# A decode step of attention plus a gated MLP on one core: the weight rows of `w_out` laid five to a lane on 128 lanes, and the remaining rows ten to a lane on 24 lanes

## The chip, the core and the metric

One NeuronCore of one Trainium2 chip. The core has a matrix engine (PE, with its weight loads PEld), a vector engine (DVE), a scalar engine (ACT), GpSimd (POOL) and SyncE (SP), which here only issues transfers. Sixteen DMA engines move data between HBM and the on-chip memory of 128 lanes. The metric is the device time of one execution in microseconds: before the change the median of three runs is 662.51 us (662.46 to 662.76).

## The reference, cut to what matters

```python
x = A_x                                   # (4, 1, 640)
xn = layernorm(x)
out = x + A(xn, k_cache, v_cache, wq, wo) + B(xn, w_in, w_sp, b_sp, w_out)

# A: attention of one new token over a cache, batch 4, 32 heads, 4096 positions, head size 128
q = (xn @ wq) by heads
p = softmax(q . k_cache * 128**-0.5)
A = (p @ v_cache) by heads, flattened, @ wo

# B: gated MLP, Fh = 864
z  = gelu(xn @ w_in)                      # w_in is 640 x 1728
z1 = z[..., :864];  z2 = layernorm(z[..., 864:])
B  = (z1 * (w_sp * z2 + b_sp)) @ w_out    # w_out is 864 x 640
```

All inputs are bf16. The two caches hold 268 MB; all weights together hold 14 MB.

## The kernel before

**Tiles.** The caches are cut into 16 tiles each, `i` = 0 to 15 (a group of eight heads and one batch). Such a tile is 128 lanes of 32768 bf16 numbers, 8.39 MB: K tiles have two buffers (`kp`), V tiles have one (`vp`). Below, K0 is the first K tile, V0 the first V tile, and so on. The weights use the same buffers: `wq` takes the first K buffer's turn, and `w_sb` the V buffer's first turn. `w_sb` holds `w_in` (columns 0 to 8639 of each lane) and behind it `w_out`.

**Transfers.** All large transfers are issued by SP, on one queue, in one order: `w_out` (L109), `wq` (L114), `w_in` (L121), four small transfers for the rest of `w_out` (L123), K0 (L139); then K1, V0 (L145) and the later tiles in turn, and `wo` (L159) last. A tile's transfer is issued when its buffer is free: K(i+2) when the PE has summed the second half of K(i) (`sums(i, 1)`, L475), V(i) when `weighted(i-1)` (L568) has read the V tile before. V0 takes the buffer of `w_sb`, so it is issued only when the MLP has used `w_out` for the last time.

**The MLP.** `gmlp()` runs once, before the loop over the tiles. It multiplies `w_in` by the transposed `xn` into `zT` (L317, 70 matmuls), applies gelu and the layernorm on DVE and ACT, and ends in `yT` (L405): seven blocks of up to 128 rows by 4 batches. Then `add_out` (L216) adds `yT` times `w_out` into `out_ps`, with four matmuls of 160 columns for each block. For this, row f of `y` must lie on the lane on which row f of `w_out` lies. The first 768 rows of `w_out` lie six to a lane (row 6p + k on lane p); `w_in`'s columns are read with a stride of six to match. The other 96 rows lie six to a lane on 16 lanes, loaded in four transfers of four lanes each; `yT`'s last block is turned to that layout by six matmuls with parts of the unit matrix (`ye_ps`, L408) and one copy (`yE`, L416).

**The loop.** For each tile, DVE multiplies a half of K(i) by q (`product`, L449), adds the two halves of the head size (`fold`, L463), and PE sums the rest into `s_ps` (`sums`, L475). DVE reduces it (L486), finds the maxima, ACT takes the exponentials (L542), DVE spreads them (`pm`, L553), and PE multiplies them by V (L568).

**Order.** From `stage_q(0)` and `gmlp()` on, the code stands in a block whose order is kept as written for PE, DVE, ACT and SP (`tc.manual_schedule`): all of `gmlp()` stands ahead of `product(0, 0)` on DVE and ahead of `sums(0, 0)` on PE. What stands ahead of that block, the loads of the weights and of K0 among it, is put in order by the framework's scheduler, which may change the order of the text. Waits are inserted by the framework, by the regions of the tiles that an instruction reads and writes.

Of the kernel before, what the change touches and what calls it, by code (L numbers as in the profile page):

```python
# [17 lines left out]
def kernel(  # L18
# [14 lines left out]
    nc = tc.nc  # L33
    P = nc.NUM_PARTITIONS
# [4 lines left out]
    Fh = F // 2  # L39
# [14 lines left out]
    SLOT = NC * Dh  # L54
# [9 lines left out]
    WJ = WH * Dh // P  # L64
    WW = 2
    WR = NG * ROWS
    NFF = Fh // P
    TL = 16
    TK = (Fh - NFF * P) // TL
    TE = 4  # L70
    NFC = NFF + TK
    F0 = NFF * P
    TF = TL * TK
    NZ = NFF + 1
    assert F0 + TF == Fh and TF <= P
    NQ = 4
    NO = D // NQ
    REP = GW // Bsz
# [18 lines left out]
    def v_slot(name):  # L97
# [8 lines left out]
    w_sb = v_slot("w_sb")  # L106
    w_in_sb = w_sb[:, 0 : DC * F].rearrange("p (c n) -> p c n", c=DC)
    w_out_sb = w_sb[:, DC * F : DC * F + NFC * D].rearrange("p (k n) -> p k n", k=NFC)
    nc.sync.dma_start(  # L109
        out=w_out_sb[:, 0:NFF, :], in_=B_w_out[0 : NFF * P].rearrange("(p k) n -> p k n", k=NFF)  # L110
# [11 lines left out]
    for l in range(TL // TE):  # L122
        nc.sync.dma_start(  # L123
            out=w_out_sb[:TL, NFF:NFC, :].rearrange("(e l) k n -> e l (k n)", e=TE)[:, l],
            in_=B_w_out[F0:Fh].rearrange("(e l k) n -> e l (k n)", e=TE, k=TK)[:, l],
        )

    def kv_view(cache, i):
# [34 lines left out]

    ident = const.tile([P, P], BF16)
    make_identity(nc, ident[:])
    ident_f = const.tile([P, P], FP32)
    nc.gpsimd.tensor_copy(out=ident_f[:], in_=ident[:])
    eps_tile = const.tile([P, 1], FP32)
# [13 lines left out]
    for i in range(NSTAT):  # L182
# [5 lines left out]
        out=rstd[:], in_=mv[:, 1:2], func=ACT.Sqrt, bias=eps_tile[:Bsz], scale=1.0  # L188
# [3 lines left out]
        out=xn_bf,  # L192
# [9 lines left out]
    for c in range(DC):  # L202
        nc.tensor.transpose(
            out=xnT_ps[:, c, :], in_=xn_v[:, c, :], identity=ident[:Bsz, :Bsz]
# [3 lines left out]
        out=xnT_r[:], in_=xnT_ps[:, :, :, None].to_broadcast([P, DC, Bsz, REP])  # L208
# [5 lines left out]
    def add_out(lhsT, rhs, start=False, stop=False):  # L214
# [14 lines left out]
        out=own[:], in_=ident_f[:].rearrange("p (h l) -> p h l", h=HT), axis=AX.X, op=ALU.add  # L229
# [4 lines left out]
        out=pick[:, :, GW - HT : GW],  # L234
        in_=ident_f[:].rearrange("p (j h c) -> p c h j", c=CB, h=HT),
# [5 lines left out]
        out=row_head_f[:],  # L241
        in_=ident_f[:WR, :WR].rearrange("p (g b h) -> p g h b", g=NG, h=HT),
# [5 lines left out]
        out=row_head[:],  # L248
        in_=row_head_f[:].rearrange("p g h -> p (g h)")[:, :, None].to_broadcast([WR, WH, WL]),
# [3 lines left out]
        out=row_batch_f[:],  # L253
        in_=ident_f[:WR, :WR].rearrange("p (g b h) -> p b g h", g=NG, h=HT),
# [12 lines left out]
    for t in range(2):  # L267
        for c in range(DC):
            for j in range(CG):
                n = CG * t + j  # L270
                nc.tensor.matmul(  # L271
                    out=q_ps[t][GW * j : GW * (j + 1), :],
                    lhsT=xnT_r[:, c].rearrange("p b r -> p (b r)"),
                    rhs=wq_t[:, c, n * NW : (n + 1) * NW],
                    start=(c == 0),
                    stop=(c == DC - 1),
                )
        nc.scalar.copy(out=q_rows[:, t, :], in_=q_ps[t][:])
    for t in range(2):
        qT_ps = ps_m.tile([P, HQ, CG, Bsz, REP], BF16, tag="m", name="qT_ps")  # L280
        for n in range(HQ):
            nc.tensor.transpose(  # L282
                out=qT_ps[:, n].rearrange("p j b r -> p (j b r)"),
                in_=q_rows[:, t, n * Dh : (n + 1) * Dh],
# [24 lines left out]
    def gmlp():  # L309
        zz, gw, gt, gz, sq = (gm[n] for n in ("zz", "gw", "gt", "gz", "sq"))  # L310
        zT = ps_pv.tile([P, 2, NZ, Bsz], FP32, tag="pv", name="zT")
        for t in range(2):
            f1 = t * Fh + F0
            w_t = w_in_sb[:, :, t * Fh : f1].rearrange("p c (f k) -> p c k f", k=NFF)
            for k in range(NZ):
                for c in range(DC):
                    nc.tensor.matmul(  # L317
                        out=zT[: P if k < NFF else TF, t, k, :],
                        lhsT=w_t[:, c, k, :] if k < NFF else w_in_sb[:, c, f1 : f1 + TF],
                        rhs=xnT[:, c, :],  # L320
                        start=(c == 0),
                        stop=(c == DC - 1),
                    )
        nc.vector.tensor_copy(out=zz[:, :, 0:NFF, :], in_=zT[:, :, 0:NFF, :])
        nc.vector.tensor_copy(out=zz[:TF, :, NFF:NZ, :], in_=zT[:TF, :, NFF:NZ, :])
        nc.vector.tensor_tensor(out=gw, in0=zz, in1=zz, op=ALU.mult)
        nc.vector.tensor_scalar(
            out=gw, in0=gw, scalar1=0.044715, scalar2=1.0, op0=ALU.mult, op1=ALU.add
        )
        nc.vector.tensor_tensor(out=gw, in0=gw, in1=zz, op=ALU.mult)  # L330
        nc.scalar.activation(
            out=gt, in_=gw, func=ACT.Tanh, scale=math.sqrt(2.0 / math.pi)
        )
        nc.vector.tensor_scalar(
            out=gt, in0=gt, scalar1=1.0, scalar2=0.5, op0=ALU.add, op1=ALU.mult
        )
        nc.vector.tensor_tensor(out=gz, in0=zz, in1=gt, op=ALU.mult)
        nc.vector.tensor_tensor(out=sq, in0=gz[:, 1, :, :], in1=gz[:, 1, :, :], op=ALU.mult)

        s_ps = ps_m.tile([1, 2, NZ, Bsz], FP32, tag="m", name="ln_ps")  # L340
        for n, src in enumerate((gz[:, 1, :, :], sq)):
            nc.tensor.matmul(
                out=s_ps[:, n, :, :], lhsT=ones_col[:], rhs=src, start=True, stop=True
            )
        st, ac = gm["st"], gm["ac"]
        mean_t = st[:, 0:Bsz]
        ex2_t = st[:, Bsz : 2 * Bsz]
        var_t = st[:, 2 * Bsz : 3 * Bsz]
        rst_t = st[:, 3 * Bsz : 4 * Bsz]
        tmp_t = st[:, 4 * Bsz : 5 * Bsz]  # L350
        nc.vector.tensor_reduce(
            out=st[:, 0 : 2 * Bsz].rearrange("a (n b) -> a n b", b=Bsz),
            in_=s_ps[:].rearrange("a n k b -> a n b k"),
            axis=AX.X,
            op=ALU.add,
        )
        nc.vector.tensor_scalar(
            out=st[:, 0 : 2 * Bsz],
            in0=st[:, 0 : 2 * Bsz],
            scalar1=1.0 / float(Fh),  # L360
            scalar2=None,
            op0=ALU.mult,
        )
        nc.vector.tensor_tensor(out=tmp_t, in0=mean_t, in1=mean_t, op=ALU.mult)
        nc.vector.tensor_tensor(out=var_t, in0=ex2_t, in1=tmp_t, op=ALU.subtract)
        nc.scalar.activation(
            out=rst_t, in_=var_t, func=ACT.Sqrt, bias=eps_tile[:1], scale=1.0
        )
        wsp_t = work.tile([1, 1], FP32, name="wsp_t")
        nc.vector.tensor_copy(out=wsp_t[:], in_=wsp_bf[:])  # L370
        bsp_t = work.tile([1, 1], FP32, name="bsp_t")
        nc.vector.tensor_copy(out=bsp_t[:], in_=bsp_bf[:])
        nc.vector.reciprocal(out=rst_t, in_=rst_t)
        nc.vector.tensor_scalar(
            out=ac[:, 0:Bsz], in0=rst_t, scalar1=wsp_t[:, 0:1], scalar2=None, op0=ALU.mult
        )
        nc.vector.tensor_tensor(out=tmp_t, in0=ac[:, 0:Bsz], in1=mean_t, op=ALU.mult)
        nc.vector.tensor_scalar(
            out=ac[:, Bsz : 2 * Bsz],
            in0=tmp_t,  # L380
            scalar1=-1.0,
            scalar2=bsp_t[:, 0:1],
            op0=ALU.mult,
            op1=ALU.add,
        )
        ac_ps = ps_m.tile([P, 2 * Bsz], FP32, tag="m", name="ac_ps")
        nc.tensor.matmul(
            out=ac_ps[:], lhsT=ones_row[:], rhs=ac[:], start=True, stop=True
        )
        ac_sb = work.tile([P, 2 * Bsz], FP32, name="ac_sb")  # L390
        nc.scalar.copy(out=ac_sb[:], in_=ac_ps[:])
        nc.vector.tensor_tensor(
            out=sq,
            in0=gz[:, 1, :, :],
            in1=ac_sb[:, None, 0:Bsz].to_broadcast([P, NZ, Bsz]),
            op=ALU.mult,
        )
        nc.vector.tensor_tensor(
            out=sq,
            in0=sq,  # L400
            in1=ac_sb[:, None, Bsz : 2 * Bsz].to_broadcast([P, NZ, Bsz]),
            op=ALU.add,
        )
        yT = work.tile([P, NZ, Bsz], BF16, name="yT")
        nc.vector.tensor_tensor(out=yT[:], in0=gz[:, 0, :, :], in1=sq, op=ALU.mult)  # L405
        ye_ps = ps_m.tile([TL, TK, Bsz], FP32, tag="m", name="ye_ps")
        for k in range(TK):
            nc.tensor.matmul(  # L408
                out=ye_ps[:, k, :],
                lhsT=ident[:TF, :TF].rearrange("p (f k) -> p k f", k=TK)[:, k, :],  # L410
                rhs=yT[:TF, NFF, :],
                start=True,
                stop=True,
            )
        yE = work.tile([TL, TK, Bsz], BF16, name="yE")
        nc.scalar.copy(out=yE[:], in_=ye_ps[:])  # L416
        for k in range(NFC):
            if k < NFF:
                add_out(yT[:, k], w_out_sb[:, k, :])
            else:  # L420
                add_out(yE[:, k - NFF], w_out_sb[:TL, k, :])
# [347 lines left out]
```

## Time and profile before

| what | value |
|---|---|
| median of 3 runs | 662.51 us |
| profiled execution, span | 661.1 us |
| DVE busy | 491.6 us (74%) |
| PE busy | 295.4 us (45%) |
| ACT busy | 34.4 us (5%) |
| POOL busy | 2.1 us |
| moved by DMA | 282.55 MB, mean 427 GB/s |
| `product` L449 | 32 x 8688 ns |
| `fold` L463 | 31 x 4410 ns |
| K tiles, issue to landing, median | 39.6 us |
| V tiles, issue to landing, median | 33.7 us |

The profile is one execution; its span is 1.4 us under the median of the runs. A page of the profile gives busy times, a row of forty slices of the span, the chain of work that ended last, and groups of instructions. The timeline lists instructions by their start; "issue" of a transfer is the instruction on SP, not the movement of data. A landing is the moment when the last byte's completion is seen. In a timeline row the columns are start, duration, engine (SPq is SP's sequencer), line, operation, output <- input, count, and in brackets the idle time before and what ended it.

### The profile page before, as it was taken

The numbers are of one execution on the slowest core, as the hardware profiler recorded it, in microseconds if no ns is written. First come the engines' busy times: TensorE is split into PE (matmuls) and PEld (weight loads), VectorE is DVE, ScalarE is ACT, GpSimd is POOL, SyncE is SP. The second block draws the span as 40 slices with busy tenths as digits, with TensorE's granted clock in tenths as the row PEclk, the third lists the DMA queues.
The fourth block names the chain that finished last, engine by engine and source line by source line (L and its number), as shares of the span: only waits on it lengthen the run. The fifth ranks groups of instructions, "written<-read, shape, count | busy, mean of one in ns | idle before, by whom it ended". The sixth has DMA issues, their size and how long they took to land.

```text
span 661.1 us, 4720 instructions
## 1 busy us (share of the span) xinstructions
PE 295.4 (45%) x2099; PEld 127.9 (19%) x2099; DVE 491.6 (74%) x222; ACT 34.4 (5%) x94; POOL 2.1 (0%) x15
## 2 busy tenths in 40 slices
PE   0513464536426253552625344362634507263656
PEld 0301121212112021220202112120211202031223
DVE  1249999959597795959779569986959699695851
ACT  0300000000000000000000000000000000000000
POOL 1000000000000000000000000000000000000000
PEclk9756676876858687675868757787775768777688
DMA  8999999999999999999999999999999999999996
GB/s 377 456 428 444 428 417 441 429 436 441 436 420 433 432 429 445 440 421 432 424 436 441 440 425 432 420 441 436 437 428 437 425 432 429 440 432 437 432 406 275
DMA packets 5712, 282.55 MB, mean 427 GB/s; under 512 B 680, under 2 KB 812, under 8 KB 1084
## 3 DMA queue, kind: packets, MB, share of 16 engines
q1 hardware_dynamic: 5664, 282.24, 98.9%
q8 instruction: 16, 0.26, 0.2%
q14 instruction: 4, 0.03, 0.0%
q10 hardware_dynamic: 28, 0.01, 0.0%
HBM read 282.24 MB, written 0.01 MB: 427 GB/s over the span
## 4 chain that ended last, share of the span: by engine, by line
DMA 51%; DVE 37%; PE 9%; issue 2%; ACT 1%; SPq 0%; DVEq 0%; ACTq 0%
DMA k_nat<-in_A_k_cache_dram 47%; DVE k_nat L449 22%; DVE k_nat L463 11%; PE s_ps L475 8%; DMA wo<-in_A_wo_dram 4%; DVE s_sb L486 3%; DMA w_sb<-in_B_w_out_dram 1%; ACT p L542 1%; PE pv L568 1%; DVE m L495 1%; PE mT L500 0%; DVE nm L505 0%; DVE pm L553 0%; SPq L159 0%; PE out_ps L216 0%
## 5 line engine op out<-in xcount | busy, mean ns | idle before, releaser
L449 DVE TENSOR_TENSOR k_nat<-k_nat,qbc 128x16384 bf16<-128x16384 bf16 x32 | 278.0, 8688 | 97.8 <-DMA k_nat<-in_A_k_cache_dram 97.8
L475 PE MATMUL s_ps<-k_nat,ident 128*128 128x512 bf16 x528 | 184.8, 528 | 139.3 <-DVE k_nat L463 139.3
L463 DVE TENSOR_TENSOR k_nat<-k_nat 128x8192 bf16<-128x8192 bf16 x31 | 136.7, 4410 | 0.0
L475 PEld LDWEIGHTS <-ident 128*128 128x128 bf16 x528 | 65.3, 129 | 248.3 <-DVE k_nat L463 123.3
L500 PE MATMUL mT<-ident_f,m 128*1 128x128 f32 x16 | 5.9, 366 | 160.0 <-DVE m L495 160.0
L568 PE MATMUL pv<-v_nat,pm 128*32 128x512 bf16 x960 | 56.1, 387 | 0.8 <-DVE pm L553 0.8
L486 DVE TENSOR_REDUCE s_sb<-s_ps 128x128 f32<-128x1024 f32 x32 | 39.0, 1218 | 5.4 <-PE s_ps L475 5.4
L500 PEld LDWEIGHTS mT<-ident_f,m 128*1 128x1 f32 x16 | 1.3, 79 | 167.8 <-DVE m L495 156.2
L568 PEld LDWEIGHTS <-pm 128*32 128x32 bf16 x1024 | 27.1, 100 | 34.3 <-issue 8.5
L553 DVE TENSOR_TENSOR pm<-p,own_c 128x2048 bf16<-128x2048 bf16 x16 | 19.6, 1225 | 15.3 <-ACT p L542 15.3
L542 ACT ACTIVATE p<-s_sb,nb 128x256 bf16<-128x256 f32 x16 | 8.1, 508 | 394.1 <-DVE nb_h L524 394.1
L591 PE MATMUL o_ps<-e,pick 128*32 128x128 f32 x128 | 17.0, 276 | 11.2 <-ACT e L578 11.2
L591 PEld LDWEIGHTS o_ps<-e,pick 128*32 128x32 f32 x128 | 12.7, 109 | 18.7 <-ACT e L578 18.7
L578 ACT COPY e<-pv 128x512 f32<-128x512 f32 x16 | 9.4, 586 | 68.1 <-PE pv L568 60.6
L287 DVE COPY qT<-qT_ps 128x64 bf16<-128x64 bf16 x2 | 0.4, 224 | 15.5 <-PE qT_ps L282 15.5
L516 PE MATMUL nb_ps<-nm,ones_row 1*128 1x8 f32 x32 | 9.2, 359 | 6.0 <-DVE nm L505 6.0
L505 DVE TENSOR_REDUCE nm<-mT 1x8 f32<-1x128 f32 x16 | 4.5, 279 | 7.5 <-PE mT L500 7.5
L516 PEld LDWEIGHTS nb_ps<-nm,ones_row 1*128 1x128 f32 x32 | 7.7, 298 | 10.6 <-DVE nm L505 9.9
L271 PE MATMUL q_ps<-wq,xnT_r 128*32 128x512 bf16 x40 | 4.3, 609 | 11.2 <-DMA wq<-in_A_wq_dram 11.2
L443 ACT CAST qbc<-qbc_ps 128x128 bf16<-128x128 f32 x16 | 4.3, 266 | 92.3 <-PE qbc_ps L435 92.3
L608 PE MATMUL den<-ones_col,acc_h 128*32 128x1 f32 x8 | 1.0, 194 | 16.6 <-DVE acc_h L601 16.6
L495 DVE TENSOR_REDUCE m<-s_sb 128x1 f32<-128x256 f32 x16 | 6.7, 420 | 0.5
(92 smaller groups left out, 70.7 us busy)
## 6 DMA issues: line engine op xcount, KB each, us to landing
wq<-in_A_wq_dram SPq DMA_DIRECT2D x1, 5120.0 KB, 16.3
wo<-in_A_wo_dram SPq DMA_DIRECT2D x1, 2560.0 KB
w_sb<-in_B_w_in_dram SPq DMA_DIRECT2D x1, 2160.0 KB, 20.9
wo<-in_A_wo_dram SPq DMA_DIRECT2D x1, 1760.0 KB
w_sb<-in_B_w_out_dram SPq DMA_DIRECT2D x1, 960.0 KB
wo<-in_A_wo_dram SPq DMA_DIRECT2D x1, 640.0 KB, 25.5
k_nat<-in_A_k_cache_dram SPq DMA_DIRECT2D x16, 39.6
v_nat<-in_A_v_cache_dram SPq DMA_DIRECT2D x15, 33.7
```

The lines of the kernel that those rows point to most:

```text
L449: nc.vector.tensor_tensor(out=part(i, u), in0=part(i, u), in1=qbcs[i][:, None, :].to_broadcast([P, UC, Dh]), op=ALU.mult,)
L463: nc.vector.tensor_tensor(out=t[:, :, 0:HD2], in0=t[:, :, 0:HD2], in1=t[:, :, HD2:Dh], op=ALU.add)
L475: nc.tensor.matmul(out=sums_ps[i][:, c : c + SC], lhsT=ident[:], rhs=t[:, c : c + SC, g * RW : (g + 1) * RW], start=(g == 0), stop=(g == n ...
L486: nc.vector.tensor_reduce(out=scores[i][:, u * UC : (u + 1) * UC], in_=sums_ps[i][:], axis=AX.X, op=ALU.add,)
L495: nc.vector.tensor_reduce(out=m1[:], in_=scores[i][:], axis=AX.X, op=ALU.max)
L500: nc.tensor.transpose(out=mT[:], in_=maxes[i][:], identity=ident_f[:])
L516: nc.tensor.matmul(out=nb_ps[:], lhsT=ones_row[:], rhs=maxes[i][:], start=True, stop=True)
L542: nc.scalar.activation(out=probs[i][:], in_=scores.pop(i)[:], func=ACT.Exp, bias=maxes.pop(i)[:], scale=scale_qk, accum_out=accs[hg][:, b ...
L553: nc.vector.tensor_tensor(out=pm[:], in0=probs.pop(i)[:] .rearrange("p (n c) -> p n c", c=CB)[:, :, None, :] .to_broadcast([P, NB, HT, CB] ...
L568: nc.tensor.matmul(out=pvs[i][j * GW : (j + 1) * GW, :], lhsT=pm[:, n, :, :].rearrange("p h c -> p (h c)"), rhs=v_nat[:, n * CB : (n + 1) ...
L578: nc.scalar.copy(out=es[i][:], in_=pvs.pop(i)[:].rearrange("p (c d) -> p c d", d=Dh))
L591: nc.tensor.matmul(out=o_ps[hg // NG][own_rows(hg), :], lhsT=pick[:, c, GW - HT - HT * b : 2 * GW - HT - HT * b], rhs=e[:, c, :], start=(b ...
```

## The change

Of the 864 rows of `w_out`, 640 lie five to a lane on 128 lanes. The other 224, and the 16 rows ahead of them once more, lie ten to a lane on 24 lanes, loaded in four transfers of six lanes each. The 16 rows that are loaded twice get the weight zero in the turned `yE`. `yT` still has seven blocks, but now the last two (rows 640 to 767 and 768 to 863) are turned: 10 x 2 matmuls instead of 6, with parts of a matrix `sel` (zeros, the unit matrix, zeros), which POOL writes into the unused end of the buffer of `w_sb`. `add_out` runs for 5 + 10 blocks instead of 6 + 6.

```diff
-    NFF = Fh // P
-    TL = 16
-    TK = (Fh - NFF * P) // TL
-    TE = 4
+    NFF = 5
+    TL = 24
+    TK = 10
+    TE = 6
     NFC = NFF + TK
     F0 = NFF * P
-    TF = TL * TK
-    NZ = NFF + 1
-    assert F0 + TF == Fh and TF <= P
+    NZ = -(-Fh // P)
+    TF = Fh - (NZ - 1) * P
+    OV = TL * TK - (Fh - F0)
+    IL = P + OV
+    IW = (NZ - NFF - 1) * P + TL * TK
...
     for l in range(TL // TE):
         nc.sync.dma_start(
             out=w_out_sb[:TL, NFF:NFC, :].rearrange("(e l) k n -> e l (k n)", e=TE)[:, l],
-            in_=B_w_out[F0:Fh].rearrange("(e l k) n -> e l (k n)", e=TE, k=TK)[:, l],
+            in_=B_w_out[Fh - TL * TK : Fh].rearrange("(e l k) n -> e l (k n)", e=TE, k=TK)[:, l],
         )
...
+    sel = w_sb[:, SLOT - IW : SLOT]
+    nc.gpsimd.memset(sel[:, 0:IL], 0.0)
+    nc.gpsimd.tensor_copy(out=sel[:, IL : IL + P], in_=ident[:])
+    nc.gpsimd.memset(sel[:, IL + P : IW], 0.0)
...
             for k in range(NZ):
+                a = (k - NFF) * P
+                n = TF if k == NZ - 1 else P
                 for c in range(DC):
                     nc.tensor.matmul(
-                        out=zT[: P if k < NFF else TF, t, k, :],
-                        lhsT=w_t[:, c, k, :] if k < NFF else w_in_sb[:, c, f1 : f1 + TF],
+                        out=zT[:n, t, k, :],
+                        lhsT=w_t[:, c, k, :]
+                        if k < NFF
+                        else w_in_sb[:, c, f1 + a : f1 + a + n],
...
-        nc.vector.tensor_copy(out=zz[:, :, 0:NFF, :], in_=zT[:, :, 0:NFF, :])
-        nc.vector.tensor_copy(out=zz[:TF, :, NFF:NZ, :], in_=zT[:TF, :, NFF:NZ, :])
+        nc.vector.tensor_copy(out=zz[:, :, 0 : NZ - 1, :], in_=zT[:, :, 0 : NZ - 1, :])
+        nc.vector.tensor_copy(out=zz[:TF, :, NZ - 1, :], in_=zT[:TF, :, NZ - 1, :])
...
         for k in range(TK):
-            nc.tensor.matmul(
-                out=ye_ps[:, k, :],
-                lhsT=ident[:TF, :TF].rearrange("p (f k) -> p k f", k=TK)[:, k, :],
-                rhs=yT[:TF, NFF, :],
-                start=True,
-                stop=True,
-            )
+            for w in range(2):
+                n = (P, TF)[w]
+                a = P * (1 - w) + k
+                nc.tensor.matmul(
+                    out=ye_ps[:, k, :],
+                    lhsT=sel[:n, a : a + TK * (TL - 1) + 1 : TK],
+                    rhs=yT[:n, NFF + w, :],
+                    start=(w == 0),
+                    stop=(w == 1),
+                )
```

In the changed kernel the lines behind these stand up to 14 lower: `product` is L463, `fold` L477, `sums` L489, the K loads L142, the small `w_out` transfers L126.

## Prediction

> **What bounds the kernel now.** I read the page first: its slices, its queue and its chain of waits.
>
> ```profile
> DMA  8999999999999999999999999999999999999996
> GB/s 377 456 428 444 428 417 441 429 436 441 436 420 433 432 429 445 440 421 432 424 436 441 440 425 432 420 441 436 437 428 437 425 432 429 440 432 437 432 406 275
> ...
> q1 hardware_dynamic: 5664, 282.24, 98.9%
> ...
> DMA 51%; DVE 37%; PE 9%; issue 2%; ACT 1%; SPq 0%; DVEq 0%; ACTq 0%
> ```
>
> The 16 DMA engines are busy in every slice and 98.9% of the span is packets of SP's one queue. DVE and PE stand in the chain only because DMA's backlog is not drawn as work; DVE is busy 74%. The kernel is one stream of bytes: whatever leaves the DMA engines without work is paid in full, and whatever doesn't is free. In the chain, K3 lands at 140.79 us and K5 at 218.19, with four tiles in between: 77.40 / 4 = 19.35 us for a tile of 8.389 MB, 27.1 GB/s for each engine. So the question is whether each tile is issued before the one ahead of it has run out. SP's timeline answers it (issue, duration):
>
> ```profile
> 2.16 3.76 SPq L123 DMA_DIRECT2D w_sb<-in_B_w_out_dram  x4
> 5.96 16.17 SPq L139 DMA_DIRECT2D k_nat<-in_A_k_cache_dram  x2
> 35.70 0.33 SPq L145 DMA_DIRECT2D v_nat<-in_A_v_cache_dram  x1
> 76.89 0.33 SPq L139 DMA_DIRECT2D k_nat<-in_A_k_cache_dram  x1
> 95.04 0.33 SPq L145 DMA_DIRECT2D v_nat<-in_A_v_cache_dram  x1
> 107.95 0.33 SPq L139 DMA_DIRECT2D k_nat<-in_A_k_cache_dram  x1
> ```
>
> K0 lands at 43.21 (chain). With 19.35 for a tile, K1 runs out at 62.6, V0 at 81.9 and K2 at 101.3; the packet records put the last packet of V0 on the slowest engine at 81.7. V0 is issued 27 us ahead of its turn, K2 (76.89) only 4.8 us ahead, V1 6.2 us: the cushion is thinnest at K2. What sets K2's issue is seen in the timeline:
>
> ```profile
> 23.85 3.73 PE L317 MATMUL zT<-xnT_r,w_sb 128*128 128x4 bf16 x70 [0.88 <-DMA w_sb<-in_B_w_out_dram]
> ...
> 33.38 0.19 DVE L405 TENSOR_TENSOR yT<-gm_t 128x28 bf16<-128x28 f32 x1
> 33.63 0.26 PE L408 MATMUL ye_ps<-yT,ident 96*16 96x4 bf16 x4 [0.92 <-DVE yT L405]
> ...
> 34.68 0.96 PE L216 MATMUL out_ps<-w_sb,yE 16*4 16x160 bf16 x24
> ...
> 43.24 8.69 DVE L449 TENSOR_TENSOR k_nat<-k_nat,qbc 128x16384 bf16<-128x16384 bf16 x1 [9.67 <-DMA k_nat<-in_A_k_cache_dram]
> ...
> 56.31 8.69 DVE L449 TENSOR_TENSOR k_nat<-k_nat,qbc 128x16384 bf16<-128x16384 bf16 x1
> ...
> 66.04 4.42 DVE L463 TENSOR_TENSOR k_nat<-k_nat 128x8192 bf16<-128x8192 bf16 x1
> ```
>
> ```profile
> 70.52 6.34 PE L475 MATMUL s_ps<-k_nat,ident 128*128 128x512 bf16 x16 [7.48 <-DVE k_nat L463]
> ```
>
> Two things to see. The MLP's very first matmul (L317) waits for the small `w_out` transfers, although it reads only `w_in`: all waits for `w_sb` stand on the first instruction that reads it. And DVE, done with the MLP at 33.57, idles 9.67 us for K0, then works without a break until K2's issue, 33.65 us after 43.24 (two products, two folds, one reduction, and sums of 6.34 us).
>
> **The change, part by part.** What matters most is not in the diff. The order in which the two programs are built differs on SP's queue:
>
> ```
> before: w_out 128x3840, wq, w_in, w_out 4x3840 (four times), K0, K1, V0, ...
> after:  w_out 128x3200, wq, w_in, K0, w_out 6x6400 (four times), K1, V0, ...
> ```
>
> In the changed program the first small transfer waits for `w_in`'s landing (no small one did before); the scheduler lets K0 go ahead of it. L326 (L317 before) still waits for all four, and `gmlp()` still stands ahead of `product(0, 0)` on DVE.
>
> (1) Bytes. The main transfer loses 128 rows: on each engine 8 x 1,280 B = 10,240 B, 0.38 us. The small ones grow from 16 x 7,680 B to 24 x 12,800 B. In the packet records of before the 16 small packets lie four each on four engines, and these finish K0 at 42.8 to 43.0, the others at 41.4 to 41.7: 1.13 us as worked out (30,720 B at 27.1 GB/s). The trace has no transfer of six lanes. Bounds: four engines as before, 6 x 0.473 = 2.83 us on each, or all 16, at most 2 x 0.473 = 0.95. I take a lane to an engine, as the four lanes did: six engines, 51,200 B, 1.89 us. The Trainium skill, "DMA: Bandwidth & Descriptors", section "Why a DMA increments its semaphore by 16 and not by 1", speaks against this shape: a transfer runs on the largest number of engines up to 16 that divides its outermost size, here six, so ten engines get none of these bytes; it gives the 1.89 us too, and four engines in before agree with it. If these bytes alone counted, the busiest engine would carry 1.89 - 1.13 - 0.38 = 0.38 us more.
>
> (2) When they land. K0's stream ends at 43.21 - 1.13 - 0.38 = 41.7; the small ones behind it on six engines at 41.7 + 1.89 = 43.6 (bounds 42.6 and 44.5). So L326 starts at 43.6 instead of 23.85. SP itself is free in time: the small issues wait for `w_in`, which lands about 22, take 0.58 us each (median of L123), and K1 is issued by 25, long before 41.7.
>
> (3) The MLP. From L317's start to `yT`'s end before: 33.57 - 23.85 = 9.72 us; counts and sizes on this path stay (70 matmuls, seven blocks). So `yT` ends at 53.3 and `product(0, 0)` starts there, not at 43.24: 10.1 us late. Behind `yT`, PE has 14 more turning matmuls (six took 0.3 us: +0.7) and 60 instead of 48 of `add_out` (24 in 0.96: +0.5): V0 is issued 2.13 + 1.2 = 3.3 us behind `yT`, at 56.7. The earliest engine ends K1 at 41.7 - 0.3 + 19.35 = about 60.7, so these matmuls, and V0, are covered by 4 us; without the cover they would cost 1.2. POOL's two fills and a copy (rows of 0.21 to 0.28 us: 0.7 in all) delay `ident_f` from 1.9 to 2.6, hidden until `wq` lands (17.5).
>
> (4) K2. Issue at 53.35 + 33.65 = 87.0. Of this the sums (6.34) vary with the granted clock, 4.96 to 6.54 in the rows of L475: bounds 85.6 and 87.2; I take 86.7. V0 has run out at 80.4 on ten engines and at 82.3 on six, so the queue is empty. Restart: the first transfer of the program, issued at 0.73, has its first packets at 1.76 to 2.41 on the 16 engines (packet records), 1.0 to 1.7 us later; the first packets then took up to 1.2 us where 0.29 is usual, so 2.2 is the upper end. With 1.7 for the slowest engine, K2 starts at 88.4 instead of 81.7: 6.7 us late. The Trainium skill, same page, section "Specifications", states about 0.6 us to the first byte on this path; with that the loss would be 5.6. The row of this case decides.
>
> (5) Is more lost later? DVE is 10.1 us late, the stream 6.7. V1, issued 95.04 + 10.1 = 105.1, has until K2 ends at 107.7: 2.6 us, covered with about one to spare behind a restart. K3 at 118.1 has until 127.1, V2 at 136.2 until 146.4. Before, DVE is ready at 133.2 and waits 7.71 us for K3; after, it is ready at 143.3 and K3 lands at 147.5, so it has caught up. The end (`wo`, 25 us on the queue) moves with the stream. The gap also levels the engines: those that lagged by 1.13 us start K2 with the rest, which I have in by counting the slowest engine on both sides.
>
> Sum: 661.1 + 6.7 = 667.8 for a profiled span; the runs lie 1.4 above it: 669.2. I say 669.0, as a random stall of 0.6 to 0.8 us that most engines show once no longer falls on engines that lag.
>
> **Rivals.**
>
> *Every tile is late.* If V1 too misses its turn (one us of cover) and those behind it, the stream carries DVE's whole delay: 10.1 us, 672.6. Against it: 9 us of cover at K3. It decides if restart or sums take 1 us more. 7%.
>
> *No wait at all; not slower.* The small transfers don't wait behind K0, because the engines take them from the queue with or ahead of K0's packets. Point: K2's issue may slip 81.7 - 1.4 - 76.9 = 3.4 us without loss, so L326 must start by 43.6 - (10.1 - 3.4) = 36.9. Then only the bytes count: +0.38 us, 662.9. For it: K0 is issued only 20 us ahead of them. Against it: before, all small packets run ahead of K0's on their engines, and K1, issued during K0, starts when K0's packets end. 6%.
>
> *Balance wins.* If in that case the bytes fell evenly on 16 engines, the lag of 1.13 us of the four engines would go too: 662.5 - 1.1 = 661.4. That is within 0.2%; the 2% that I leave for it also cover a gain over 0.2%, for which the trace names no further source.
>
> **How the numbers follow.** 0.2% is 1.3 us, about what this measurement can tell from no change. My forecast, one gap ahead of K2, has 85%: 669.0, its own range 666.8 to 671.0 (sums 1.4 us shorter and restart 0.6 shorter; six small packets to an engine and a restart of 2.2). The rivals take 7, 6 and 2%. Range 666.4 to 671.4. Slower 0.92, same 0.06, faster 0.02.
>
> **What would show it.** In the profile after: the small `w_out` transfers issued behind K0 and landing near 43.6; L326 at 43.6; L463's first row at 53.3 behind the MLP, not behind DMA; K2 issued near 87; the DMA row's sixth slice (82.6 to 99.2) with a third of it empty, near 290 GB/s, and no other such slice. Wrong would be: L326 near 23, or a full sixth slice, or a second hole at V1.

## The result, and the profile after

The changed kernel takes 670.25 us (median of 4 runs, 669.65 to 670.7) against 662.63 for the kernel before in the same comparison: a ratio of 1.0114, 95% interval 1.0102 to 1.0126, 7.6 us slower. The profiled execution has a span of 668.8 us against 661.1, 7.7 more.

The page of the kernel after: the head, the two DMA rows of the 40 slices (16.7 us each), and SP's queue.

```profile
span 668.8 us, 4775 instructions
...
DMA  8999789999999999999999999999999999999996
GB/s 372 437 454 424 333 357 400 436 439 435 436 439 436 435 439 429 431 432 423 436 439 427 427 436 439 432 435 435 432 431 432 428 435 428 435 439 432 435 404 273
...
q1 hardware_dynamic: 5680, 282.26, 97.8%
```

The fifth and sixth slices (67 to 100 us) have fallen; by the packet records they hold 2.9 and 3.9 us of idle time for each DMA engine. The seventh (400 against 441) holds none: a packet counts in the slice in which it starts, and behind the hole the engines start their packets nearly together. From the eighth on the rows read as before. The queue's packets take 97.8% of 668.8, 654.1 us, against 98.9% of 661.1, 653.8: hardly more work, 7.4 us more idle. A view by stretches (us, then busy time and count by engine, granted clock, DMA share, GB/s) shows where. First before, then after:

```profile
75.00:82.00 7.00, 2.60 (x9) 0.98 (x7) 6.41 (x5) 0.00 (x0) 0.00 (x0) 0.74 1.03 440
82.00:88.00 6.00, 2.32 (x7) 0.85 (x8) 5.33 (x5) 0.79 (x3) 0.00 (x0) 0.50 1.09 461
88.00:95.00 7.00, 7.00 (x77) 2.92 (x75) 7.00 (x1) 0.27 (x1) 0.00 (x0) 0.88 0.97 421
```

```profile
75.00:82.00 7.00, 2.11 (x6) 0.73 (x7) 7.00 (x3) 0.00 (x0) 0.00 (x0) 0.53 0.67 290
82.00:88.00 6.00, 4.34 (x12) 1.46 (x10) 6.00 (x1) 0.00 (x0) 0.00 (x0) 0.70 0.45 153
88.00:95.00 7.00, 0.93 (x3) 0.57 (x3) 6.50 (x5) 0.00 (x0) 0.00 (x0) 0.57 0.74 318
```

The view puts a packet's whole share where the packet starts, so packets of 2.4 us blur the edges; the packet records give the hole exactly. (They name no DMA engine; a packet is counted to the engine whose packet before it ended just when it starts.) V0's last packet ends between 79.72 and 81.58, K2's first starts between 87.32 and 88.28. Added over the 16 engines and divided by 16, 6.85 us of idle lie between 75 and 95 us, where the kernel before has none. SP's timeline of after shows why:

```profile
2.43 0.65 SPq L142 DMA_DIRECT2D k_nat<-in_A_k_cache_dram  x1
22.49 2.98 SPq L126 DMA_DIRECT2D w_sb<-in_B_w_out_dram  x4
25.59 0.35 SPq L142 DMA_DIRECT2D k_nat<-in_A_k_cache_dram  x1
56.01 0.33 SPq L148 DMA_DIRECT2D v_nat<-in_A_v_cache_dram  x1
86.37 0.33 SPq L142 DMA_DIRECT2D k_nat<-in_A_k_cache_dram  x1
104.48 0.33 SPq L148 DMA_DIRECT2D v_nat<-in_A_v_cache_dram  x1
```

K0 is issued at 2.43 and the four transfers of the tail 20 us behind it; K2 is issued at 86.37, 4.8 us after the last packet of V0; before it was issued 4.6 us ahead of that (76.89 against 81.48). The link between the two, in the timeline of after:

```profile
43.56 3.15 PE L326 MATMUL zT<-xnT_r,w_sb 128*128 128x4 bf16 x70 [20.97 <-DMA w_sb<-in_B_w_out_dram]
...
52.52 0.19 DVE L416 TENSOR_TENSOR yT<-gm_t 128x28 bf16<-128x28 f32 x1
52.62 8.68 DVE L463 TENSOR_TENSOR k_nat<-k_nat,qbc 128x16384 bf16<-128x16384 bf16 x1
```

PE waits 20.97 us for the tail, and DVE's first product starts behind `yT` with no wait for a DMA in its brackets: K0 has been there for 11 us.

### The profile page after: what moved, and what is told of

Its sections match the earlier page's. It is cut to its first block, busy times and chain, and to the rows that moved or that the text cites. A ratio compares the mean times of both kernels' runs of the same rounds, so it can differ in the third digit from the quotient of the medians.

```text
span 668.8 us, 4775 instructions
## 1 busy us (share of the span) xinstructions
PE 298.3 (45%) x2125; PEld 129.3 (19%) x2125; DVE 491.4 (73%) x222; ACT 34.5 (5%) x94; POOL 2.6 (0%) x18
## 3 DMA queue, kind: packets, MB, share of 16 engines
q1 hardware_dynamic: 5680, 282.26, 97.8%
## 4 chain that ended last, share of the span: by engine, by line
DMA 49%; DVE 37%; PE 11%; issue 2%; ACT 1%; SPq 1%; DVEq 0%; ACTq 0%
DMA k_nat<-in_A_k_cache_dram 40%; DVE k_nat L463 22%; DVE k_nat L477 10%; PE s_ps L489 9%; DMA wo<-in_A_wo_dram 4%; DMA w_sb<-in_B_w_in_dram 3%; DMA w_sb<-in_B_w_out_dram 3%; DVE s_sb L500 3%; ACT p L556 1%; PE pv L582 1%; DVE m L509 1%; PE zT L326 0%; PE mT L514 0%; DVE nm L519 0%; SPq L126 0%
## 5 line engine op out<-in xcount | busy, mean ns | idle before, releaser
L463 DVE TENSOR_TENSOR k_nat<-k_nat,qbc 128x16384 bf16<-128x16384 bf16 x32 | 278.0, 8688 | 87.3 <-DMA k_nat<-in_A_k_cache_dram 87.3
L489 PE MATMUL s_ps<-k_nat,ident 128*128 128x512 bf16 x528 | 189.7, 539 | 130.1 <-DVE k_nat L477 130.1
L477 DVE TENSOR_TENSOR k_nat<-k_nat 128x8192 bf16<-128x8192 bf16 x31 | 136.7, 4409 | 0.0
L489 PEld LDWEIGHTS <-ident 128*128 128x128 bf16 x528 | 66.6, 131 | 242.7 <-DVE k_nat L477 125.0
L582 PE MATMUL pv<-v_nat,pm 128*32 128x512 bf16 x960 | 54.6, 380 | 0.8 <-DVE pm L567 0.8
L326 PE MATMUL zT<-xnT_r,w_sb 128*128 128x4 bf16 (+1 forms) x70 | 3.1, 183 | 21.0 <-DMA w_sb<-in_B_w_out_dram 21.0
```

What stands on the lines that cost most here:

```text
L463: nc.vector.tensor_tensor(out=part(i, u), in0=part(i, u), in1=qbcs[i][:, None, :].to_broadcast([P, UC, Dh]), op=ALU.mult,)
L477: nc.vector.tensor_tensor(out=t[:, :, 0:HD2], in0=t[:, :, 0:HD2], in1=t[:, :, HD2:Dh], op=ALU.add)
L489: nc.tensor.matmul(out=sums_ps[i][:, c : c + SC], lhsT=ident[:], rhs=t[:, c : c + SC, g * RW : (g + 1) * RW], start=(g == 0), stop=(g == n ...
L582: nc.tensor.matmul(out=pvs[i][j * GW : (j + 1) * GW, :], lhsT=pm[:, n, :, :].rearrange("p h c -> p (h c)"), rhs=v_nat[:, n * CB : (n + 1) ...
```

## The experiments

The theory "queue": the whole loss comes from the tail's transfers standing behind K0 on SP's queue. Rivals: "shape" (the ten-row layout, its bytes, its extra matmuls and copies) and "wait" (SP held up by the tail's wait for `w_in`). Each kernel was timed beside the kernel before, which took 662.6 us in every comparison (median 662.59 to 662.64).

**K0 ahead of the tail in the old layout** (edit of the kernel before):

```diff
-    for l in range(TL // TE):
-        nc.sync.dma_start(out=w_out_sb[:TL, NFF:NFC, :]..., in_=B_w_out[F0:Fh]...)
...
     load_k(0)
+    for l in range(TL // TE):
+        nc.sync.dma_start(out=w_out_sb[:TL, NFF:NFC, :]..., in_=B_w_out[F0:Fh]...)
```

> Kernel before with one edit: K0 is issued ahead of the four small w_out transfers, all else as it was. Theory 'queue': the small ones land near 43.0 us, the MLP starts there, product(0, 0) at 52.3 (the MLP took 9.15 us from zT to yT in the changed kernel), K2 is issued at 86.0, 0.4 earlier than in the changed kernel, and the time is 669.9 (669.2 to 670.4). Rival 'shape': 662.6, as before. Rival 'wait' (the loss comes from SP waiting for w_in's landing with the tail's transfers): 662.6 too, since no transfer of the tail waits for w_in here.

671.04 us, 1.0127 (1.0113 to 1.0141). The tail's issue, the first matmul and K2's issue, from its timeline:

```profile
2.87 3.79 SPq L157 DMA_DIRECT2D w_sb<-in_B_w_out_dram  x4
```

```profile
43.40 3.72 PE L316 MATMUL zT<-xnT_r,w_sb 128*128 128x4 bf16 x70 [20.83 <-DMA w_sb<-in_B_w_out_dram]
```

```profile
86.45 0.33 SPq L133 DMA_DIRECT2D k_nat<-in_A_k_cache_dram  x1
```

The order alone, with the old layout, old bytes and old matmuls, costs 8.4 us, 0.8 more than the change itself and 0.6 over the top of its expected range. No transfer of the tail waits for `w_in` here: they are issued from 2.87 us on. "Shape" and "wait" fall as the cause.

**The tail in one transfer, new layout** (`TE = 6` becomes `TE = 24`). Built so, the tail goes without a wait for `w_in` and ahead of K0: it is issued at 2.17 us, K0 at 2.93.

> Changed kernel, but the tail of w_out (24 lanes of ten rows) goes in one transfer of 24 lanes instead of four of six. Everything else of the change stays: the layout, the extra matmuls, POOL's work, the rows loaded twice. The built order on SP is then that of the text (tail ahead of K0), without a wait for w_in. Theory 'queue' (the whole loss comes from the tail's transfers standing behind K0): the first zT matmul starts near 23.5 us, no stretch of empty DMA queues at 82 to 88, and only bytes count: -0.38 for the smaller main transfer, -1.13 for the four lagging engines, +0.95 for two packets of 12,800 B on each of twelve engines: 0.6 us under before, 662.0. Rival 'shape' (the loss comes from the ten-row layout, its bytes or its extra work): near 670, as the changed kernel.

664.1 us, 1.0022 (1.0013 to 1.0031).

```profile
23.36 2.83 PE L326 MATMUL zT<-xnT_r,w_sb 128*128 128x4 bf16 x70 [0.31 <-DMA w_sb<-in_B_w_in_dram]
```

```profile
78.02 0.33 SPq L142 DMA_DIRECT2D k_nat<-in_A_k_cache_dram  x1
```

The MLP starts at 23.36, K2 is issued in time, and 6.1 of the 7.6 us are back, with all the extra matmuls and POOL's work still there: these are hidden. But it should have been 0.6 under before and is 1.5 over. In the packet records K0's first packet takes 0.25 to 1.2 us longer on all 16 engines while the tail is written, and the tail's own packets are slow too: 1.28 us for each engine between 20 and 30 us, about half of it on K0's packets, against none in the kernel before.

**K0 cut in two, the tail between the parts** (half, and three quarters, ahead of it):

```diff
+        cut = (NC // 2) * Dh if i == 0 else SLOT
-        nc.sync.dma_start(out=t[:], in_=kv_view(A_k_cache, i))
+        nc.sync.dma_start(out=t[:, 0:cut], in_=kv_view(A_k_cache, i)[:, 0:cut])
...
+        load_rest()
+        load_k(1)
         stage_q(0)
         gmlp()
```

`load_rest` issues the other part of K0; `load_k(1)` moves there from above. The other kernel has `NC * 3 // 4`.

> Changed kernel with K0 cut in two transfers: the first half of its columns ahead of the tail's four transfers, the second half behind them, ahead of K1. The tail still waits for w_in. Theory 'queue': the tail lands after half a tile's stream, zT starts at 33.8, yT ends at 43.0, just when the second half of K0 lands (43.3), so DVE loses nothing: K2 issued near 77, no empty queues, 663.0 (0.4 over before for the bytes on the busiest engines). Rivals 'shape' and 'wait': near 670.

664.15 us, 1.0022 (1.0013 to 1.0032).

> As k0_half, with three quarters of K0 ahead of the tail and one quarter behind. Theory 'queue': zT starts at 38.6, past the 36.9 us from which the prediction had a loss begin; product(0, 0) starts at 47.8, K2 is issued at 81.4 and the slowest engine starts it at 83.6 instead of 81.7: 1.9 us lost, or up to 0.9 more since the changed kernel lost that much after K2: 664.5 to 665.4. Rivals 'shape' and 'wait': near 670. If the loss is in proportion to the delay of the MLP without a cushion, 668.

665.48 us, 1.0044 (1.0031 to 1.0058), 0.1 over the top of its expected range. The first matmul and K2's issue, first with a half, then with three quarters:

```profile
34.04 3.15 PE L334 MATMUL zT<-xnT_r,w_sb 128*128 128x4 bf16 x70 [11.79 <-DMA w_sb<-in_B_w_out_dram]
```

```profile
76.23 0.33 SPq L143 DMA_DIRECT2D k_nat<-in_A_k_cache_dram  x1
```

```profile
38.93 3.15 PE L334 MATMUL zT<-xnT_r,w_sb 128*128 128x4 bf16 x70 [15.77 <-DMA w_sb<-in_B_w_out_dram]
```

```profile
81.36 0.33 SPq L143 DMA_DIRECT2D k_nat<-in_A_k_cache_dram  x1
```

This is the cushion, measured at three points. With the MLP at 34.0 the queue never runs dry (no idle at 75 to 95 us), though the tail waits for `w_in` as in the changed kernel; at 38.9 the hole is 1.8 us; at 43.6 it is 6.85. So 4.6 us of delay cost 5.0 us of idle, about one for one; by that slope the cushion ends at 37 or so. The half still lies 1.1 us over its expectation: in its packet records the engines idle 2.3 us on the mean between 640 us and the last packet of `wo`, against 1.3 before. That is where the lag of six engines, 1.9 us, would be paid; the kernel was not varied further to show it.

**DVE's first product ahead of the MLP** (the tail still behind K0):

```diff
         stage_q(0)
+        product(0, 0)
         gmlp()
...
-            product(i, 0)
+            if i > 0:
+                product(i, 0)
```

> Changed kernel, the tail still behind K0, but DVE's first product (8.69 us, on K0, which lands at 41.7) stands ahead of the MLP. Theory 'queue', by way of DVE's order: product(0, 0) runs 41.8 to 50.5, the MLP's DVE work behind it takes 5.8 us (from the copy of zT to yT in the changed kernel), K2 is issued at 41.8 + 33.65 + 5.8 = 81.2, V0 at 59.6, and the slowest engine starts K2 at 83.3 instead of 81.7: 664.2 to 665.2. If the late tail costs by something else than DVE's order (the PE's order, the buffer of w_sb), the time stays near 670.

665.78 us, 1.0049 (1.0033 to 1.0064).

```profile
41.74 8.69 DVE L463 TENSOR_TENSOR k_nat<-k_nat,qbc 128x16384 bf16<-128x16384 bf16 x1 [18.74 <-DMA k_nat<-in_A_k_cache_dram]
```

```profile
43.64 3.15 PE L326 MATMUL zT<-xnT_r,w_sb 128*128 128x4 bf16 x70 [20.78 <-DMA w_sb<-in_B_w_out_dram]
```

```profile
80.78 0.33 SPq L142 DMA_DIRECT2D k_nat<-in_A_k_cache_dram  x1
```

The MLP starts as late as in the changed kernel, yet 4.5 us are back, because DVE uses the wait. So the late tail costs by way of DVE's order. The time is 0.6 over the top of the expected range: idle is only 0.4 us ahead of V0 and 0.4 ahead of K2, but each of the two restarts has slow first packets (0.5 and 0.7 us for each engine, packet records).

**The tail on ACT's queue** (`nc.sync` becomes `nc.scalar` in the tail's loop):

> Changed kernel with the tail's four transfers issued by ACT on its own queue (behind the casts of q, still behind w_in's landing), SP's queue without them. Theory 'queue' (a transfer waits for those ahead of it on its own queue, while an engine alternates between queues): each of the four packets of an engine waits for about one K0 packet of 2.42 us, so the tail lands by 36, the MLP loses DVE little or nothing: 662.8 to 663.4. If the engines take packets in the order of issue whatever the queue, the tail lands at 43.5 and the time is 670.

672.84 us, 1.0144 (1.013 to 1.0158): both expectations miss.

```profile
23.17 2.95 ACTq L126 DMA_DIRECT2D w_sb<-in_B_w_out_dram  x4
...
45.97 3.15 PE L326 MATMUL zT<-xnT_r,w_sb 128*128 128x4 bf16 x70 [22.84 <-issue]
```

In the packet records the engines alternate between the queues packet by packet, but the 4 B packet by which each transfer reports itself done takes a turn of its own. So a small transfer costs two packets of K0: the first three small packets of an engine start near 28.8, 34.1 and 39.4 (5.3 us apart: 2 x 2.42 + 0.48). The fourth starts near 42.3, because SP's turn ahead of it is only K0's own 4 B report. The tail's bytes are all in at 42.93, just as in the changed kernel. But the fourth report waits for a packet of K1, 2.4 us more: the reports come at 45.13 to 45.34, the transfer counts as landed at 45.76, and L326, for which the view names no releaser, starts at 45.97 instead of 43.56. A second queue was no way past the long transfer here.

**The new layout's four transfers, issued in time** (the tail's loop moved up, ahead of the load of `wq`):

> Changed kernel with its four transfers of six lanes unchanged, but issued right behind w_out's main transfer, ahead of wq and w_in: K0 is behind them again, and w_in waits for them (they land near 6 us, while wq streams until 17). Everything else as in the changed kernel. Theory 'queue': the first zT matmul at 23 to 24 us, no empty queues at 82 to 88, only the 0.38 us more bytes on the busiest engines, and up to 0.5 at the start for wq's later issue: 662.9 to 663.6. Rival 'shape': 670.

665.2 us, 1.0047 (1.0033 to 1.0061); the five runs spread from 664.46 to 666.87. The hole at K2 is gone, so the order is the cause once more; 1.6 us over expectation are left. `wq` is issued only behind the four transfers, and by the view by stretches the start moves less (2 to 12 us: 364 GB/s, 421 before):

```profile
4.21 0.44 SPq L123 DMA_DIRECT2D wq<-in_A_wq_dram  x1
```

```profile
2.00:12.00 10.00, 0.68 (x9) 0.48 (x9) 2.71 (x10) 1.58 (x2) 1.14 (x7) 1.00 0.92 364
```

10 us x 57 GB/s at 430 GB/s are 1.3 us, and K0's first packet starts at 23.25 instead of 21.84. Why the runs spread is open.

**The old layout's tail in one transfer** (`TE = 4` becomes `TE = 16`):

> Kernel before with its tail (16 lanes of six rows) in one transfer of 16 lanes instead of four of four. If the end is set by the engines that carry most bytes: 7,680 B on each of 16 engines instead of 30,720 B on four, the busiest have 0.85 us less: 661.8, faster than both kernels. If the lag of four engines is hidden anyway: 662.6.

663.94 us, 1.0017 (1.0009 to 1.0026): slower, not faster. Again K0's first packets are slow on all engines (0.99 us for each between 20 and 30 us). Two readings were left: that writing the tail to 16 neighbouring lanes holds up everyone, or that balanced engines are slower for another reason. Three kernels tell them apart.

**Four neighbouring lanes in each of the four transfers** (kernel before; `(e l)` becomes `(l e)` on both sides of the tail's transfers):

> Kernel before, with each of the four small transfers going to four neighbouring lanes (0 to 3, 4 to 7, ...) instead of lanes four apart. Same bytes, same engines, same order. The two kernels with one transfer for the tail came out 1.3 to 1.5 us over before instead of under it, and in their traces K0's first packet on all 16 engines took up to 1.2 us longer while the tail was being written. Theory 'lanes' (four neighbouring lanes take no more than one engine's rate, about 27 GB/s, whoever writes): a small packet takes 4 x 0.29 = 1.16 us, the four engines lag by 4.5 us instead of 1.13, the first zT matmul starts near 27, and the time is 662.6 + 3.4 = 666.0. Rival 'engines in step' (balanced engines are slower for another reason): packets of 0.29 us and 662.6.

663.61 us, 1.0015 (1.0006 to 1.0024). The tail's 0.29 us packets take up to 0.79, and K0's first packets on the other engines 0.5 us longer, in all 0.65 us for each engine: same bytes, same engines, same order, other lanes. The direction is that of "lanes"; the size is not: 1.0 us slower than before, where packets of 1.16 us would have given 3.4.

**One row to a lane on 96 lanes, and three rows to a lane on 32** (kernel before; `TL = 96, TE = 96`, and `TL = 32, TE = 8`):

> Kernel before with the last 96 rows of w_out one to a lane on 96 lanes, in one transfer: six packets of 1,280 B on each of 16 engines. The turning of yT becomes one matmul with the unit matrix, add_out has 7 blocks instead of 12. Theory 'lanes': the writes spread over all groups of lanes, K0's first packets are not slowed, no engine carries more than another: 0.85 us under before, 661.7 to 661.9, faster than both kernels. Rival 'engines in step': 663.9, as the other two kernels whose tail goes in one transfer.

> Kernel before with the last 96 rows three to a lane on 32 lanes, in four transfers of eight lanes four apart: four packets of 3,840 B on each of eight engines. Theory 'lanes' with the lag of the busiest engines counting: 15,360 B instead of 30,720 B on the busiest, 0.57 us under before, 662.0. If the lag of a few engines costs nothing: 662.6. Rival 'engines in step' (the less lag, the slower): over 662.6.

663.31 us, 1.001 (1.0001 to 1.0019), and 663.18, 1.001 (1.0002 to 1.0019). Spread over more lanes, the tail slows K0's first packets by 0.15 us for each engine and not at all, where 16 lanes in one transfer cost 0.99. So the slow first packets go with the lanes that are written, and not with balanced engines. The times are another matter: both miss what "lanes" expected (661.7 to 661.9, and 662.0) and lie 0.7 and 0.55 us over before, as "engines in step" had it, though the 96 lanes are not at its 663.9. What takes that time stays open: the traced run of the 96 lanes, the shortest of eleven, shows none of it. No gain shows from the lag of four engines, 1.1 us, that the one takes away and the other halves. None of the versions tried beats the kernel before.

## Why the prediction was right

Direction, mechanism and place came out, and the time, 670.25, lies in the range of 666.4 to 671.4 and of the forecast's own 666.8 to 671.0, 1.25 over its point of 669.0. Step by step:

- *The order on SP's queue, which the diff does not show.* As built. The old layout with this order alone is as slow (671.04), the new layout without it is not (664.1, 665.2).
- *(1) Bytes, (2) landing.* Six engines with four packets each, 479 ns a packet (0.473 worked out); L326 at 43.56 (43.6). The Trainium skill's count of engines for an outermost size of six, cited in the prediction, agrees.
- *(3) The MLP.* `yT` ends at 52.71 (53.3): the 70 matmuls took 3.15 us instead of 3.73. V0 is issued at 56.01 (56.7), 4.4 us before K1 runs out on the first engine (60.40, packet records), so the extra matmuls are covered.
- *(4) K2.* Issued at 86.37 (86.7), sums of 6.45 us.

```profile
79.89 6.45 PE L489 MATMUL s_ps<-k_nat,ident 128*128 128x512 bf16 x16 [9.06 <-DVE k_nat L477]
```

- *(5) Later tiles.* V1 at 104.48, in time; there is no second hole. "Every tile is late" did not come, "no wait at all" neither: the queue is in order. The point of 36.9 us, from which a late MLP costs, lies between the measured 34.0 (no hole) and 38.9 (1.8 us).
- *The term that was too small* is the loss at K2 in (4): 6.7 us forecast, 7.6 measured. The slowest engine starts K2 at 88.28 instead of 81.48, 6.8 us later, as forecast, and the first packets start 0.95 to 1.9 us after the issue, much as the 1.0 to 1.7 taken from the program's start. But the slowest engine was the wrong one to count. On the mean over the engines the start moves by 7.1 us; and the first packets then take 3.04 us instead of 2.52. So the mean end of K2's first packet moves from 82.98 to 90.59, by 7.61, and this is what the last packet of `wo` (657.13 to 664.91, 7.78) and the runs (7.62) show. It reads as if what the engines lose together counts and the lag of a few does not. The kernels with 96 and 32 lanes fit that, the kernel with half of K0 ahead of the tail does not, so it is argued and not shown. The 0.2 us that I took off for the levelled engines do not show: the end moves no less than K2. The Trainium skill's 0.6 us to the first byte ("DMA: Bandwidth & Descriptors", section "Specifications") lies under the least, 0.95 us, that this restart shows.
- *The sign that came out otherwise.* The hole was to lie in the sixth slice alone, near 290 GB/s. It begins at 79.7 us on the first engine to run out, so it is shared by the fifth (333) and the sixth (357).
- *Packet times.* The prediction's packet times for the ends of K0 and V0 (41.4 to 43.0, and 81.7) are 0.2 us late on the timeline's clock: 81.7 is 81.48, and K2's lead before was 4.6 us, not 4.8. Differences between packet times are not touched, but (4) takes 81.7 from a time that starts at the issue: on one clock its 6.7 would have been 6.9.

## What to carry to other kernels

A kernel bound by one stream of transfers is judged by one question: is each transfer issued before the one ahead of it has run out, and by how much. Read the order of issue of the program as built, not as written: here one small transfer that the scheduler let fall behind a long one held up, through an engine's fixed order, an issue 40 us later, and it cost one for one only past the cushion. Before a tail is re-laid out, ask what waits for it first.

## What the runs showed of the hardware that was not expected

- Where a small transfer is written matters to everyone. 123 KB to 16 neighbouring lanes in one transfer cost each of the 16 engines 0.99 us, nearly all of it on K0's first packets, which go to all 128 lanes; 307 KB to 24 lanes cost 1.28, about half of it on K0's; the same 123 KB over 32 lanes, in transfers of lanes four apart, or over 96 lanes cost 0 and 0.15. The Trainium skill, "SBUF — State Buffer", section "Door 1: The DMA port swizzle", says that four neighbouring lanes share one port of about 27 GB/s and lanes 0 to 15 reach four. By that, 123 KB need an estimated 1.13 us on four ports, and the 0.99 us is of that size; for four neighbours in a transfer it would give an estimated 1.16 us a packet, and 0.29 to 0.79 were measured.
- On an engine with two queues the packets took turns one by one, and the 4 B packet that reports a transfer done took a turn of its own. Small transfers beside 64 KiB packets so came 5.3 us apart, and the last was reported 2.4 us after its bytes.
- An empty queue cost more than its latency: 0.95 to 1.9 us from K2's issue to the first packet on an engine, and 0.5 us more on that packet (3.04 us against 2.52).
